# Earlier scale steps, sooner operands and one split in the first token-MLP of an interleaved GFNet and Mixer kernel

## The chip, the cores and the metric

The kernel runs on one core of a Trainium2 chip. The metric is the device time of one execution in microseconds (us). Three runs of the kernel before took 987.86, 980.19 and 978.45 us; their median is 980.19.

A core has five engines that run side by side, each through its own queue in order: TensorE (PE, matrix products, with PEld for loading its weights), VectorE (DVE), ScalarE (ACT), GpSimd (POOL) and SyncE (SP), which here only issues transfers. An engine waits for another through semaphores, and everything queued behind a waiting instruction waits too.

## The reference

Four layers with residuals follow each other on x of 2048 tokens by 640 channels: a spectral filter, a token-mixing MLP, and the same two again with the same weights.

```python
def _A_ref(x, w_r, w_i):
    B, S, D = x.shape
    X = rfft2(x, axes=(-2, -1))
    X = X * (w_r + 1j * w_i)
    return irfft2(X, s=(S, D), axes=(-2, -1))

def _B_ref(x, w1, b1, w2, b2):
    h = _layernorm(x, axis=-1)                  # (1, 2048, 640)
    u = jnp.einsum("bsd,sf->bdf", h, w1) + b1   # F = 1728
    u = _gelu(u)
    y = jnp.einsum("bdf,fs->bds", u, w2) + b2
    return y.transpose(0, 2, 1)

x = A_x
x = x + _A_ref(_layernorm(x, axis=-1), A_w_r, A_w_i)
x = x + _B_ref(_layernorm(x, axis=-1), B_w1, B_b1, B_w2, B_b2)
x = x + _A_ref(_layernorm(x, axis=-1), A_w_r, A_w_i)
x = x + _B_ref(_layernorm(x, axis=-1), B_w1, B_b1, B_w2, B_b2)
```

## The kernel before

The spectral filter is done as matrix products with tables (tM, tD, tS, tI). Products that need float32 are made from float16 parts: an operand is scaled by a power of two and split into a high half (written by ACT) and a low half, the rest (written by DVE as one scalar_tensor_tensor of source, scale and high half). One product is then three passes: high by high, high by low, low by high.

The change is all in `b1st`, the token-MLP of the first round. It has two parts. The first contracts the 2048 tokens with w1 into 1728 hidden rows, in 14 weight tiles of 128 rows (`NFT`; the last half-filled); the second contracts the hidden rows with w2 into 2048 tokens, in 16 tiles (`NJ`). Tiles are numbered through: 0 to 13 are w1, 14 to 29 are w2.

Tiles 0 to 3 of w1 are done plainly (`both`: 48 steps of two matmuls of 128x320, the three passes). The other ten are five pairs (4 and 5, 6 and 7, and so on), and each pair is done in the manner of Strassen: seven products of block sums in place of eight. The table `ops` lists 35 such products as (pair, name): first A11 and A12 of the first and second pair, then S1, S2, S4, S3, A22 of both, then all seven of the third, fourth and fifth pair. The weight operand of each comes from raw w1 blocks and their sums X (`ssum`), the activation operand from blocks and sums T1 to T4 of h (`tsum` forms them in place on DVE, `thi` writes the high half on ACT, `tlo` the low half on DVE). `product(n)` issues 24 matmuls. `work(n)` issues what stands around it: it evicts product n−1, splits the weight of product n+3 (`hi` on ACT, `lo` on DVE, with a store of the split weight on POOL's queue for the second round), forms the sum for product n+4, and then runs the closures listed in `todo[n]`. `work(-4)` to `work(-1)` run inside `both` of tile 3.

A weight scale is a power of two from the sum of squares. `wload(m)` loads a tile (two transfers of raw weights, by SP). `scan1(m)` is ACT's Square with a sum per partition (`junk<-raw`). `scale1(m)` is a generator with three steps, each taken by `step(m)`: first DVE adds the partial sums up into `sqb`; second PE multiplies `ones` with it, which puts the sum on all partitions; third five small DVE operations make the power of two (`s1p`, `c1p` for pairs, `st`, `ct` for tiles of w2). The second and third step of a pair stand at the table `mms` inside a product, those of the second pair in `both` at j == 32.

For w2, `wsplit(m)` writes `wh` on ACT and `wl` on DVE, in two halves of 896 columns. Tile 14 is split from `todo`, tile m+1 during product m. Each product of w2 is evicted as a row x (128 tokens by 640), whose layernorm for the next spectral layer follows: statistics on DVE, `r` and `nb` on POOL, `z` on ACT, folds on POOL and DVE (`eo`, `f`), a split (`fh`, `fl`) and a product with tM. Between the products stand the split of the next tile, scans and scale steps, and loads, at fixed places of the inner loop (`i`).

Order: each engine's instructions run in the order of its queue. From the start of `b1st` until after the last `ulo`, `self.pin` is true, and every instruction is kept in the order in which the code is written. After that, except in the last three rows, a scheduler sets the order of each engine from its estimates. All instructions go through the wrapper `Pin`, so the profile gives them one line, L83, and they are told apart by engine and tile.

Of the kernel before, what the change touches and what calls it, by code (L numbers as in the profile page):

```python
# [21 lines left out]
NJ, NG, NFT = 16, 16, 14  # L22
# [32 lines left out]
PAIR = 4  # L55
# [35 lines left out]
class Layers:  # L91
# [965 lines left out]
    def b1st(self, li):  # L1057
# [9 lines left out]
        prod, tsum, thi, tlo, hlow, hhigh, hlows = H.prod, H.tsum, H.thi, H.tlo, H.hlow, H.hhigh, H.hlows  # L1067
# [7 lines left out]
        def step(m):  # L1075
            if m in sc:
                next(sc[m])
# [11 lines left out]
        def ssum(d, a):  # L1089
            if a == "S1":  # L1090
                X[d] = self.t(self.pX, [128, 8, 128], F32, "X", 1)
            x, y, op = {"S1": ("A21", "A22", ADD), "S2": ("S1", "A11", SUB), "S3": ("A11", "A21", SUB), "S4": ("A12", "S2", SUB)}[a]
            V.tensor_tensor(src(d, a), src(d, x), src(d, y), op=op)

        begin, rest = ("A11", "A12"), ("S1", "S2", "S4", "S3", "A22")
        ops = [(d, a) for ds, q in (((0, 1), begin), ((0, 1), rest)) for d in ds for a in q]
# [7 lines left out]
        def hi(n):  # L1104
            if 0 <= n < len(ops):
                d, a = ops[n]
                q, tag = places(n)
                wo[n] = self.t(q, [128, NJ, 128], F16, tag, 1).rearrange("p (a b) c -> p a b c", a=2)
                T.activation(wo[n][:, 0], src(d, a), AF.Identity, scale=self.s1p[:, d:d + 1])

        def lo(n):
            if 0 <= n < len(ops):
                d, a = ops[n]
                V.scalar_tensor_tensor(wo[n][:, 1], src(d, a), self.s1p[:, d:d + 1], wo[n][:, 0], op0=MUL, op1=SUB)
                nc.gpsimd.dma_start(self.ws1[d][a], wo[n])
# [12 lines left out]
        def gelu(o, x=None, **q):  # L1128
            T.activation(o, o if x is None else x, AF.Gelu_apprx_tanh, **q)

        def evict(n):
            if not 0 <= n < len(ops):
                return
            (d, a), ps = ops[n], bank[n]
            c = self.c1p[:, d:d + 1]
            if a == "A11":
                f[d] = self.t(pf, [128, 4, 320], F32, "f", 4)
            to = f[d]
            if a in ("A11", "S1"):
                for i in (0, 2) if a == "A11" else (3,):  # L1140
                    T.activation(to[:, i], ps, AF.Identity, scale=c)
            else:
                i, k = {"S2": (2, 2), "S4": (1, 2), "S3": (2, 2), "A12": (0, 0), "A22": (2, 2)}[a]
                V.scalar_tensor_tensor(to[:, i], ps, c, to[:, k], op0=MUL, op1=ADD)
            if a in ("S4", "S3"):
                i, k = (1, 3) if a == "S4" else (3, 2)
                V.tensor_tensor(to[:, i], to[:, i], to[:, k], op=ADD)

        def evicted(n):
            if n > 0 and ops[n][1] in ("S4", "A22"):  # L1150
                d, k = ops[n][0], 2 * (ops[n][1] == "A22")
                gelu(f[d][:, k:k + 2], bias=self.b1[:, d + 7 * k // 2:d + 7 * k // 2 + 1])

        def work(n, more=()):

            evict(n - 1)
            hi(n + 3)
            d, a = ops[n + 4] if 0 <= n + 4 < len(ops) else (0, "A11")
            if a in ("S1", "S3", "S4"):
                ssum(d, a)  # L1160
            lo(n + 3)
            if a == "S2":
                ssum(d, a)
            evicted(n - 1)
            for e in more:
                e()
# [4 lines left out]
        def uhi(e, i=0, k=4):  # L1171
            T.activation(U[e][:, 0, i:i + k], fu(e)[:, i:i + k], AF.Identity, scale=self.su)

        def ulo(e, i=0, k=4, c=slice(0, 128)):
            h, l = (U[e][c, q, i:i + k] for q in range(2))
            V.scalar_tensor_tensor(l, fu(e)[c, i:i + k], self.su[c], h, op0=MUL, op1=SUB)
# [46 lines left out]
        def plain(m, o, x):  # L1223
            i = SEQ[m]
            gelu(o, x, scale=self.ct[0][:, i:i + 1], bias=self.b1[:, i:i + 1])
# [33 lines left out]
        def both(ps, w):  # L1259
            for k, (i, h) in enumerate(((0, hhigh), (0, hlows), (1, hhigh))):  # L1260
                for j in every:
                    yield k * NJ + j
                    prod(ps, w[i], h, [j], start=k == 0, stop=k == 2)

        for j in both(ps, w):
            pass
        plain(2, f[5][:, 0:2], flat(ps))
        ps, w = self.big(), self.w.pop(3)
        self.wstore(3, w)
# [2 lines left out]
        todo = collections.defaultdict(list)  # L1272
        lam = lambda g, *a, **k: lambda: g(*a, **k)
        for d in range(2, 5):
            a, b, n = 2 * d + PAIR, 2 * d + PAIR + 1, 7 * d
            for m, c, q, k in ((a, 0, "S3", 3), (a, 1, "S4", 2), (b, 0, "S3", 2), (b, 1, "A22", 2)):
                todo[at[d - 2, q] - k].append(lam(self.wload, m, (c,)))
            for k, m, c in ((9, a, 0), (8, a, 1), (8, b, 0), (7, b, 1)) if d == 2 else ((11, a, 0), (10, a, 1), (9, b, 0), (7, b, 1)):
                todo[n - k].append(lam(self.scan1, m, (c,)))
            for k in (6, 5) if d > 2 else (5, 4):  # L1280
                todo[n - k].append(lam(step, a))
        one = PAIR + 2
        for q in one, one + 1:
            self.wload(q)
        todo[-4] += [lam(self.scan1, one), lam(tlo, "T1"), lam(thi, "T3")]
        todo[-3] += [lam(self.scan1, one + 1), lam(tlo, "T2")]
        todo[-2] += [lam(step, one)]
        todo[0] += [lam(tlo, "T3")]
        todo[1] += [lam(tsum, "T4", 0), lam(tsum, "T4", 1), lam(thi, "T4")]
        todo[3] += [lam(tlo, "T4")]  # L1290
        a, b = NFT, NFT + 1
        for n, m, c in ((22, a, 0), (23, b, 0), (24, a, 1), (25, b, 1), (31, a + 2, 0), (31, a + 2, 1), (32, a + 3, 0), (32, a + 3, 1)):
            todo[n].append(lam(self.wload, m, (c,)))
# [5 lines left out]
        for k, e in enumerate((0, 6, 5, 1, 2, 3)):  # L1299
            todo[25 + k].append(lam(uhi, e))  # L1300
            todo[26 + k].append(ulast if e == 6 else lam(ulo, e))
        todo[32] += [lam(self.wopen, a), lam(self.wsplit, a, (0,))]
        todo[33] += [lam(self.wsplit, a, (1,))]
        todo[34] += [lam(uhi, 4, 0, 2), lam(ulo, 4, 0, 2)]
        mms = {7 * d - 4 - (d > 2): 2 * d + PAIR for d in range(2, 5)}
        mms.update({30: a, 34: b})

        for j in both(ps, w):
            if j % 12 == 0:
                work(j // 12 - 4, todo[j // 12 - 4])  # L1310
            if j == 32:
                step(one)
                step(one)
        plain(3, f[5][:, 2:4], flat(ps))
        for n in range(len(ops)):
            if n == 5:
# [4 lines left out]
            work(n, todo[n])  # L1321
        evict(len(ops) - 1)
        evicted(len(ops) - 1)
        uhi(4, 2, 2)
        ulo(4, 2, 2)
        step(NFT + 2)
        self.pin = False
        for a in ("f", "fr", "T", "h", "ha"):
            self.pop(a)
# [48 lines left out]
        for j in range(NJ):  # L1378
# [42 lines left out]
            def sum5(a):  # L1421
                x = X[5], px5[0]
                o, x, op = (X[5], x if a < "S3" else x[::-1], ADD if a == "S1" else SUB)
                with self.after(evicted5):
                    V.tensor_tensor(o, *x, op=op)
                nc.sync.dma_start(self.ws1[5][a], o)
# [10 lines left out]
            for i, (ft, a, k) in enumerate(order):  # L1437
                if i == 14 and w5[:1] > ("",):
                    sum5(w5[0])
                if i == 20:  # L1440
                    for q in w5[1:]:
                        load5(q)
                if tail and i == NFT:
                    half(0)
                if j == NJ - 2 and i in (4, 20):
                    flush(1)
                if j >= NJ - 2 and i in (6, 12, 17):
                    next(row)
                if tail and i == 2:
                    self.wopen(0)  # L1450
                    self.wsplit(0, lo=False)
                if i in (4, 8):
                    next(steps, None)
                if j == NJ - 3 and i == 9:
                    self.wload(0)
                if i in ((6, 7) if j else (18, 19)):
                    step(m + 2)
                if i in (15, 18):
                    self.scan1(m + 3, (i // 3 - 5,))
                if i == 26 and m + 3 < NFT + NJ:  # L1460
                    step(m + 3)
                o = pss[a][:, :320]
                if not j:
                    first(o, ft, a, k)
                elif ft < NFT - 1:
                    self.mm3(o, (wh[:, ft], wl[:, ft]), (upart(ft, a, 0), upart(ft, a, 1)), ft == SEQ[0], ft == SEQ[-1])
                else:
                    mm(o, wh[:, ft], upart(ft, a, 1), start=False, stop=False)
                    mm(o, wl[:, ft], upart(ft, a, 0), start=False, stop=False)
# [722 lines left out]
```

## Time and profile before

| what | value |
|---|---|
| median of three runs | 980.19 us (978.45 to 987.86) |
| the profiled execution, its time | 984.12 us |
| its span on the core | 982.3 us |
| mean granted TensorE clock | 0.979 |
| PE busy | 934.8 us, 95% |
| DVE busy | 754.8 us, 77% |
| ACT busy | 565.5 us, 58% |
| POOL busy | 293.3 us, 30% |
| DMA moved | 179.42 MB, 183 GB/s on average |

A timeline row gives start, duration, engine, operation, out<-in with shapes, how many, and in brackets how long the engine had been idle and what ended that. Rows that say "x16" are merged. "sqTrue" and "sqFalse" are sums of squares of a pair and of a single tile. In the first token-MLP the weights of the Strassen products are called `wo`, `wh` or `wl` by the place that holds them, so there `wh<-raw` on DVE is a low half too.

### The profile page before, as it was taken

To read this page: it belongs to the slowest core of one execution; us is meant where nothing else is said; L and a number is where in the kernel's file an instruction comes from. 1 tells how busy PE (TensorE), PEld (TensorE's weight loads), DVE (VectorE), ACT (ScalarE), POOL (GpSimd) and SP (SyncE) were. 2 spreads that over 40 slices of the span, in tenths; PEclk is the share of its full clock that TensorE was granted. 3 is DMA by queue.
4 is the path that set the end of the run, shared out by engine and by line. 5 is a ranking of instruction groups with operands and counts; after the bars stand their busy time and mean duration, and the time that the engine had idled before them with its cause. 6 is when DMAs were issued, how large, how long until landed. Compare 5 with 4: busy or idle time off the path is not lost.

```text
span 982.3 us, 22469 instructions
## 1 busy us (share of the span) xinstructions
PE 934.8 (95%) x9009; PEld 691.2 (70%) x9009; DVE 754.8 (77%) x1407; ACT 565.5 (58%) x869; POOL 293.3 (30%) x496
## 2 busy tenths in 40 slices
PE   3889899999999989999999898999999999999998
PEld 2768777666677767777777686776777777777776
DVE  7979989987988956666667897889735455988885
ACT  5847879884676674555544476684433344454431
POOL 6939867311111112122223495772000000000000
PEclk9599999998999999999999999999999999999999
DMA  7856377642887685664332663674555447655411
GB/s 259 284 153 173 107 238 237 220 171 88 297 306 243 230 314 190 214 201 130 111 93 81 173 194 123 206 242 158 165 163 160 143 132 274 219 192 176 146 48 52
DMA packets 68108, 179.42 MB, mean 183 GB/s; under 512 B 8010, under 2 KB 15332, under 8 KB 68004
## 3 DMA queue, kind: packets, MB, share of 16 engines
q1 hardware_dynamic: 60820, 151.63, 47.6%
q0 software_dynamic: 7184, 26.36, 7.3%
q8 instruction: 70, 1.15, 0.5%
q14 instruction: 34, 0.28, 0.1%
HBM read 130.39 MB, written 47.58 MB: 181 GB/s over the span
## 4 chain that ended last, share of the span: by engine, by line
PE 49%; DVE 24%; ACT 9%; POOL 7%; issue 6%; DMA 5%; SPq 1%; ACTq 0%; DVEq 0%; POOLq 0%
PE ps L83 49%; DVE f L83 4%; DVE wl L83 3%; DVE st L83 3%; POOL eo L83 3%; DMA raw<-w 2%; DVE s1l L83 2%; DMA xt<-x 2%; ACT wh L83 2%; ACT junk L83 2%; ACT z L83 1%; DVE xt L83 1%; DVE Yl L83 1%; POOL xt L83 1%; POOL xl L83 1%
## 5 line engine op out<-in xcount | busy, mean ns | idle before, releaser
L83 PEld LDWEIGHTS <-wh 128*128 128x128 f16 x2298 | 222.4, 98 | 89.3 <-issue 1.7
L83 PE MATMUL ps<-u,wh 128*128 128x320 f16 x1242 | 228.5, 299 | 0.7 <-ACT wh L83 0.7
L83 PEld LDWEIGHTS <-wl 128*128 128x128 f16 x1626 | 159.9, 99 | 69.6 <-issue 5.6
L83 PE MATMUL ps<-u,wl 128*128 128x320 f16 x826 | 182.1, 299 | 0.1
L83 PEld LDWEIGHTS <-wo 128*128 128x128 f16 x924 | 90.3, 98 | 35.9 <-issue 0.9
L83 POOL TENSOR_TENSOR r<-v,mh 128x1 f32<-128x1 f32 x64 | 39.3, 613 | 147.7 <-DVE nm L83 138.4
L83 PE MATMUL ps<-tDi,Yh 128*128 128x322 f16 x320 | 72.4, 304 | 1.5 <-ACT Yh L83 1.5
L83 ACT ACTIVATE junk<-raw 128x896 bf16<-128x896 f32 (+1 forms) x60 | 59.4, 991 | 13.1 <-DMA raw<-w 11.0
L83 DVE TENSOR_TENSOR f<-eo 128x256 f32<-128x256 f32 (+1 forms) x124 | 39.0, 367 | 36.2 <-POOL eo L83 35.6
L83 POOL TENSOR_TENSOR xt<-xt,ec 128x320 f32<-128x320 f32 x64 | 53.3, 853 | 31.8 <-DVE xt L83 31.7
L83 DVE BATCH_NORM_STATS2 st<-xt 128x6 f32<-128x320 f32 x126 | 55.2, 480 | 5.1 <-DMA xt<-x 4.5
L83 PE MATMUL ps<-u,wo 128*128 128x320 f16 x420 | 58.8, 299 | 0.0
L83 ACT ACTIVATE z<-xt,nb,r 128x640 f32<-128x640 f32 x31 | 28.5, 918 | 52.5 <-POOL z L83 43.2
L83 PE MATMUL ps<-tM,f 128*128 128x128 f32 x160 | 37.6, 402 | 21.5 <-DMA xt<-x 11.4
L83 PE MATMUL ps<-tDi,Yl 128*128 128x322 f16 x192 | 56.4, 302 | 1.4 <-DVE Yl L83 1.4
L83 DVE SCALAR_TENSOR_TENSOR wl<-raw,s,wh 128x896 f16<-128x896 f32 (+2 forms) x43 | 48.0, 1123 | 12.6 <-ACT wh L83 12.4
L83 POOL TENSOR_TENSOR eo<-z 128x320 f32<-128x320 f32 x60 | 52.2, 892 | 17.3 <-ACT z L83 15.3
L83 PEld LDWEIGHTS ps<-tM,f 128*128 128x128 f32 x160 | 31.5, 283 | 27.3 <-DVE f L83 26.8
L83 POOL TENSOR_TENSOR xl<-ta,xh 128x642 f16<-128x642 f32 (+2 forms) x34 | 45.5, 1347 | 4.6 <-ACT xh L83 4.5
L83 ACT ACTIVATE wh<-raw,s 128x896 f16<-128x896 f32 (+2 forms) x46 | 43.7, 987 | 2.6 <-DVE s L83 1.8
L83 POOL MEMSET wl<- 64x256 f16 x2 | 0.6, 306 | 146.7 <-DMA wl<-w2A 146.7
L83 PE MATMUL ps<-hhb,wh 128*128 128x320 f16 x256 | 43.5, 299 | 0.4 <-ACT hhb L83 0.4
(257 smaller groups left out, 2222.9 us busy)
## 6 DMA issues: line engine op xcount, KB each, us to landing
xt<-x SPq DMA_DIRECT2D x79, 320.0 KB
raw<-w SPq DMA_DIRECT2D x32, 512.0 KB
w<-w SPq DMA_DIRECT2D x48, 321.0 KB
x<-xt SPq DMA_DIRECT2D x47, 320.0 KB
raw<-w SPq DMA_DIRECT2D x32, 448.0 KB
raw<-w2z SPq DMA_DIRECT2D x32, 448.0 KB
out<-xt SPq DMA_DIRECT2D x15, 320.0 KB
w1S<-wl POOLq DMA_DIRECT2D x9, 512.0 KB, 5.8
```

The costliest lines, as they stand in the source:

```text
L83: i = f(*a, **k)
```

## The change

It has four parts, and adds or removes no instruction on any engine.

1. The second pair (tiles 6 and 7). Its loads are issued before `both` of tile 2 instead of after, and the scan of tile 6 stands ahead of the eviction of tile 2 on ACT. In `both` of tile 3 `work(-4)` to `work(-1)` stand at j = 0, 12, 32, 36 instead of 0, 12, 24, 36; the first scale step of the pair and the sum S1 of the first pair are issued with `work(-3)` instead of `work(-2)` and `work(0)`; the high half of T3 comes behind the scans of tile 7, and T3's low half and T4's sums come two places sooner, T4's low half one.
2. The first scale step of the third pair comes one product sooner.
3. Both halves of tile 14 are split in `todo[32]`, where the second was in `todo[33]`.
4. The first scale step of tile 16 stands ahead of the last `uhi` and `ulo`, and its second and third step stand at i = 44 and 45 of the first product of w2 instead of 18 and 19.

```diff
-            d, a = ops[n + 4] if 0 <= n + 4 < len(ops) else (0, "A11")
+            d, a = ops[n + 4] if 0 < n < len(ops) - 4 else (0, "A11")
...
+        one = PAIR + 2
+        for q in one, one + 1:
+            self.wload(q)
         for j in both(ps, w):
             pass
+        self.scan1(one)
         plain(2, f[5][:, 0:2], flat(ps))
...
-            for k in (6, 5) if d > 2 else (5, 4):
+            for k in (6, 5) if d > 2 else (6, 4):
                 todo[n - k].append(lam(step, a))
-        one = PAIR + 2
-        for q in one, one + 1:
-            self.wload(q)
-        todo[-4] += [lam(self.scan1, one), lam(tlo, "T1"), lam(thi, "T3")]
-        todo[-3] += [lam(self.scan1, one + 1), lam(tlo, "T2")]
-        todo[-2] += [lam(step, one)]
-        todo[0] += [lam(tlo, "T3")]
-        todo[1] += [lam(tsum, "T4", 0), lam(tsum, "T4", 1), lam(thi, "T4")]
-        todo[3] += [lam(tlo, "T4")]
+        todo[-4] += [lam(tlo, "T1")]
+        todo[-3] += [lam(self.scan1, one + 1), lam(tlo, "T2"), lam(thi, "T3"), lam(step, one), lam(ssum, 0, "S1")]
+        todo[-2] += [lam(tlo, "T3")]
+        todo[-1] += [lam(tsum, "T4", 0), lam(tsum, "T4", 1)]
+        todo[1] += [lam(thi, "T4")]
+        todo[2] += [lam(tlo, "T4")]
...
-        todo[32] += [lam(self.wopen, a), lam(self.wsplit, a, (0,))]
-        todo[33] += [lam(self.wsplit, a, (1,))]
+        todo[32] += [lam(self.wopen, a), lam(self.wsplit, a)]
...
         for j in both(ps, w):
-            if j % 12 == 0:
-                work(j // 12 - 4, todo[j // 12 - 4])
             if j == 32:
                 step(one)
                 step(one)
+            if j in (0, 12, 32, 36):
+                n = {0: -4, 12: -3, 32: -2, 36: -1}[j]
+                work(n, todo[n])
...
+        step(NFT + 2)
         uhi(4, 2, 2)
         ulo(4, 2, 2)
-        step(NFT + 2)
...
-                if i in ((6, 7) if j else (18, 19)):
+                if i in ((6, 7) if j else (44, 45)):
                     step(m + 2)
```

The first place is ACT while PE works on tiles 2 and 3 of w1. Before, from the second half of T2h on (`junk` are the scans of tiles 6 and 7, `wo` and `wh` weights of the first products, `fr` the eviction of tile 2):

```order
L83 ACTIVATE T2h_3698<-hf_326_2845 128x1280
L83 ACTIVATE fr_522_3909<-ps_3968,b1s,c_74 128x640
L83 ACTIVATE junk,sqTrue_4077<-raw_4069 128x1024
L83 ACTIVATE junk,sqTrue_4077<-raw_4071 128x1024
L83 ACTIVATE T3h_3700<-hf_326_2842 128x1280
L83 ACTIVATE T3h_3700<-hf_326_2843 128x1280
L83 ACTIVATE wo_4108<-raw_3712,sp_79 128x1024
L83 ACTIVATE junk,sqTrue_4077<-raw_4073 128x1024
L83 ACTIVATE junk,sqTrue_4077<-raw_4075 128x1024
L83 ACTIVATE wh_4140<-raw_3714,sp_79 128x1024
```

and now:

```order
L83 ACTIVATE T2h_3698<-hf_326_2845 128x1280
L83 ACTIVATE junk,sqTrue_4073<-raw_3969 128x1024
L83 ACTIVATE junk,sqTrue_4073<-raw_3971 128x1024
L83 ACTIVATE fr_522_3909<-ps_3968,b1s,c_74 128x640
L83 ACTIVATE wo_4106<-raw_3712,sp_79 128x1024
L83 ACTIVATE junk,sqTrue_4073<-raw_3973 128x1024
L83 ACTIVATE junk,sqTrue_4073<-raw_3975 128x1024
L83 ACTIVATE T3h_3700<-hf_326_2842 128x1280
L83 ACTIVATE T3h_3700<-hf_326_2843 128x1280
L83 ACTIVATE wh_4168<-raw_3714,sp_79 128x1024
```

Tile 6's scans moved ahead of the eviction, and T3h from between the two tiles' scans to behind them; `wo` stands ahead of tile 7's scans in place of T3h.

The same place on DVE, with - for before and + for now (`sqb` is the sum of the second pair, `X` the sum S1 of the first pair, `qt` the first of the scale's small operations, which reads PE's result):

```order
-L83 SCALAR_TENSOR_TENSOR wo_4108<-raw_3712,sp_79,wo_4108 128x1024
+L83 SCALAR_TENSOR_TENSOR wo_4106<-raw_3712,sp_79,wo_4106 128x1024
 L83 TENSOR_TENSOR T2l_3699<-hf_326_2844,T2h_3698 128x1280
 L83 TENSOR_TENSOR T2l_3699<-hf_326_2845,T2h_3698 128x1280
-L83 SCALAR_TENSOR_TENSOR wh_4140<-raw_3714,sp_79,wh_4140 128x1024
-L83 TENSOR_REDUCE sqb_536_4144<-sqTrue_4077 128x1
+L83 TENSOR_REDUCE sqb_535_4116<-sqTrue_4073 128x1
+L83 TENSOR_TENSOR X_4118<-raw_3716,raw_3718 128x1024
 L83 TENSOR_SCALAR qt<-ps_3739 128x1
```

`sqb` now follows T2l directly, the low half of `wh` stands behind the scale's operations, and X is formed in the time between.

The second place is DVE around the last products of w1 (`wl_5390` are the two low halves of tile 14, `sqb_655` the sum of tile 15, `f` evictions):

```order
 L83 SCALAR_TENSOR_TENSOR f_5271<-ps_5321,cp_80,f_5271 128x320
 L83 SCALAR_TENSOR_TENSOR wl_5390<-raw_5016,s_73,wh_5389 128x896
+L83 SCALAR_TENSOR_TENSOR wl_5390<-raw_5088,s_73,wh_5389 128x896
 L83 SCALAR_TENSOR_TENSOR f_5271<-ps_5358,cp_80,f_5271 128x320
 L83 TENSOR_TENSOR f_5271<-f_5271 128x320
-L83 TENSOR_REDUCE sqb_655_5424<-sqFalse_5355 128x1
-L83 SCALAR_TENSOR_TENSOR wl_5390<-raw_5088,s_73,wh_5389 128x896
-L83 SCALAR_TENSOR_TENSOR f_5271<-ps_5393,cp_80,f_5271 128x320
+L83 TENSOR_REDUCE sqb_655_5426<-sqFalse_5355 128x1
+L83 SCALAR_TENSOR_TENSOR f_5271<-ps_5395,cp_80,f_5271 128x320
```

Tile 14's second low half moved ahead of an eviction, its addition and tile 15's `sqb`.

The third place is DVE at the start of the w2 stage. First the sum of tile 16 (`sqb_659`) against the low halves of tile 15 (`wl_5509`) and the last hidden rows (`u`):

```order
+L83 TENSOR_REDUCE sqb_659_5469<-sqFalse_5423 128x1
 L83 SCALAR_TENSOR_TENSOR wl_5509<-raw_5056,s_73,wh_5508 128x896
 L83 SCALAR_TENSOR_TENSOR wl_5509<-raw_5132,s_73,wh_5508 128x896
 L83 SCALAR_TENSOR_TENSOR u_554_4385<-f_5271,su,u_554_4385 128x640
-L83 TENSOR_REDUCE sqb_659_5471<-sqFalse_5421 128x1
-L83 TENSOR_REDUCE sqb_674_5579<-sqFalse_5546 128x1
```

`sqb_659` moved from behind these to ahead of them. Then the first row (`xt_5500`) against the low halves of tile 16 (`wl_5652`), where the scheduler sets the order:

```order
 L83 SCALAR_TENSOR_TENSOR wl_5652<-raw_5351,s_73,wh_5651 128x896
+L83 SCALAR_TENSOR_TENSOR xt_5500<-ps_5513,c_75,xt_5500 128x640
+L83 TENSOR_SCALAR q_671_5569<-ps_5675 128x1
 L83 SCALAR_TENSOR_TENSOR wl_5652<-raw_5353,s_73,wh_5651 128x896
-L83 SCALAR_TENSOR_TENSOR xt_5500<-ps_5513,c_75,xt_5500 128x640
-L83 TENSOR_SCALAR q_673_5578<-ps_5675 128x1
 L83 BN_STATS st_5617<-xt_5500 128x6 x2
```

The second low half of tile 16 moved from ahead of the row's eviction to between the eviction and the row's statistics. On SP the second load of tile 18 now stands ahead of the loads of tD, tS and tI, where it stood behind them. On PE the only move is the product of `ones` for tile 16, 16 matmuls later.

## The prediction

> **What bounds the kernel now.** I read the page first: the span, the busy shares and the shares of the chain that ended last.
>
> ```profile
> span 982.3 us, 22469 instructions
> PE 934.8 (95%) x9009; PEld 691.2 (70%) x9009; DVE 754.8 (77%) x1407; ACT 565.5 (58%) x869; POOL 293.3 (30%) x496
> PE 49%; DVE 24%; ACT 9%; POOL 7%; issue 6%; DMA 5%; SPq 1%; ACTq 0%; DVEq 0%; POOLq 0%
> ```
>
> TensorE (PE) is busy 95% of the span, so a reordering can win only PE's idle time or matmuls that run at half clock; 982.3 − 934.8 = 47.5 us are idle in all. The change touches one token-MLP, the first, so next come PE's waits between 175 and 400 us (us in total, times, longest), and PE by stretches (length, busy us and count of PE, PEld, DVE, ACT, POOL, then the granted clock, DMA share, GB/s).
>
> ```profile
> PE ps L83 <- DVE sqb L83: 6.1, 4, 3.2
> PE ps L83 <- ACT wh L83: 0.7, 1, 0.7
> ```
>
> ```profile
> 220.00:224.00 4.00, 2.14 (x10) 1.22 (x10) 2.73 (x10) 1.15 (x1) 0.53 (x1) 0.58 0.32 133
> 224.00:228.00 4.00, 4.00 (x18) 2.36 (x17) 2.42 (x2) 0.00 (x0) 0.53 (x1) 0.56 0.43 175
> 228.00:264.00 36.00, 35.91 (x265) 25.73 (x263) 31.95 (x31) 22.09 (x28) 4.78 (x9) 1.00 0.52 185
> 400.00:450.00 50.00, 50.00 (x409) 36.95 (x408) 30.66 (x87) 25.51 (x39) 11.29 (x24) 1.00 0.60 191
> ```
>
> The stage holds 6.8 us of waits that have a name: four times PE waited for `sqb`, the reduced sum of squares that its small matmul with `ones` spreads over the partitions to set a weight scale, and once for the high half of a weight (`wh`). A second loss is in the clock column: around the longest wait the granted clock is 0.58 and 0.56. From 400 to 450 PE never waits. So the prize lies between 218 and 354 us, and what becomes of it is settled in the w2 stage after it.
>
> **The change part by part.** It adds and removes no arithmetic; every price is a wait removed, a wait added, or a position in a queue. *First part, the second pair (tiles 6 and 7).* The timeline of before around the longest wait:
>
> ```profile
> 205.41 2.34 PE L83 MATMUL ps<-hha,wl 128*128 128x320 f16 x16
> 209.75 2.34 PE L83 MATMUL ps<-hha,wh 128*128 128x320 f16 x16
> 209.96 0.88 ACT L83 ACTIVATE fr<-ps,b1s,c 128x640 f32<-128x640 f32 x1 [1.90 <-PE ps L83]
> 210.74 1.04 ACT L83 ACTIVATE junk<-raw 128x1024 bf16<-128x1024 f32 x1
> 211.91 1.06 ACT L83 ACTIVATE junk<-raw 128x1024 bf16<-128x1024 f32 x1
> 212.96 2.41 ACT L83 ACTIVATE T3h<-hf 128x1280 f16<-128x1280 f32 x2
> 215.28 1.13 ACT L83 ACTIVATE wo<-raw,sp 128x1024 f16<-128x1024 f32 x1
> 216.32 1.04 ACT L83 ACTIVATE junk<-raw 128x1024 bf16<-128x1024 f32 x1
> 217.49 1.06 ACT L83 ACTIVATE junk<-raw 128x1024 bf16<-128x1024 f32 x1
> 217.65 2.88 DVE L83 TENSOR_TENSOR T2l<-hf,T2h 128x1280 f16<-128x1280 f32 x2
> 220.46 1.27 DVE L83 SCALAR_TENSOR_TENSOR wh<-raw,sp,wh 128x1024 f16<-128x1024 f32 x1
> 221.65 0.15 DVE L83 TENSOR_REDUCE sqb<-sqTrue 128x1 bf16<-128x4 f32 x1
> 221.86 0.16 PE L83 MATMUL ps<-sqb,ones 128*128 128x1 bf16 x1 [3.25 <-DVE sqb L83]
> 221.88 4.43 PE L83 MATMUL ps<-hha,wl 128*128 128x320 f16 x16
> 228.97 1.25 PE L83 MATMUL ps<-hha,wo 128*128 128x320 f16 x8
> ```
>
> PE arrived at 221.86 − 3.25 = 218.61. The four scans (`junk`) were long done; `sqb` was late because it stood on DVE behind T2l and a weight's low half, which had waited for ACT's T3h and `wo`. Now T3h (2.41) stands behind the scans and `wo` on ACT, and on DVE `sqb` follows T2l. How far that brings it hangs on when tiles 6 and 7 land. The landings aren't listed, but this is the DMA traffic from 200 to 220 in half-microsecond slices:
>
> ```profile
> GB/s 0 0 0 0 0 0 139 188 254 279 336 352 369 401 410 401 320 123 188 156 213 262 180 295 311 336 393 262 123 33 0 0 0 0 0 0 0 0 319 393
> ```
>
> The dip to 123 at 208.5 parts tile 6's loads from tile 7's, and nothing moves from 215 to 219, so all of tile 7 has landed by about 215. Tile 6's second half landed between the dip and 211.91, when its scan began; I take the middle, 210.2. Forward on ACT: second scan with its read-out to 211.5, eviction 212.4, `wo` 213.5; on DVE its low half (1.27) to 214.8, T2l 217.7, `sqb` 217.8, some 0.8 us ahead of PE; tile 7's last scan ends near 216.4. Bounds: none of the wait stays; or, with tile 6 at 211.91, all that slides by 1.7 us and a stall of about 1.0 stays. I take all: −3.25. The clock: the 32 matmuls on the `wl` half took 209.75 − 205.41 = 4.34 us for tile 2 and 228.97 − 221.88 = 7.09 here, with nothing waited for in between: −2.75 if the idle time that caused it is gone. Together −6.00. The rule in the Trainium skill, page "TensorE: Matmul & The Clock Gate", section "Part 1: The HAM clock gate (the "warmup" mystery)", is that the gate halves the rate only after at least one idle window of about 3.4 us, in a window that runs free. By that an idle time of 3.25 us would cost no clock and this part be worth 3.25; the stretch with 0.58 right behind that wait disagrees, so the measured 2.75 is in the sum.
>
> *T3 and T4 sooner* cost nothing on PE if DVE keeps ahead. DVE is busy 31.95 of 36 us between 228 and 264, where the first pair's products of 24 matmuls run at 4.34 × 24/32 = 3.26 us each; with PE 6 us sooner, T3l, X and the T4 sums stand ahead of the low halves that PE wants third and fourth. In order: scale steps done at 220.1, `wh` low 221.4, T3l 224.3, `wl` low 225.6; PE wants that `wl` at 228.97 − 6.0 + 2 × 3.26 = 229.5. Cover 3.9 us; if it went, the price would be what DVE is late.
>
> *Second part, one operation earlier for the third pair.*
>
> ```profile
> 263.22 1.27 DVE L83 SCALAR_TENSOR_TENSOR wl<-raw,sp,wl 128x1024 f16<-128x1024 f32 x1
> 264.42 0.15 DVE L83 TENSOR_REDUCE sqb<-sqTrue 128x1 bf16<-128x4 f32 x1
> 264.62 0.16 PE L83 MATMUL ps<-sqb,ones 128*128 128x1 bf16 x1 [0.71 <-DVE sqb L83]
> ```
>
> `sqb` stood behind a low half of 1.27; moved ahead of it and of an eviction it saves more than the wait: −0.71, all of it.
>
> *Third and fourth part, into the w2 stage.*
>
> ```profile
> 342.76 0.15 DVE L83 TENSOR_REDUCE sqb<-sqFalse 128x1 bf16<-128x2 f32 x1
> 343.10 0.17 PE L83 MATMUL ps<-sqb,ones 128*128 128x1 bf16 x1
> 345.62 5.88 PE L83 MATMUL ps<-u,wh 128*128 128x320 f16 x42 [0.70 <-ACT wh L83]
> 351.89 1.15 DVE L83 SCALAR_TENSOR_TENSOR wl<-raw,s,wh 128x896 f16<-128x896 f32 x1 [0.55 <-ACT wh L83]
> 353.76 0.21 DVE L83 TENSOR_REDUCE sqb<-sqFalse 128x1 bf16<-128x2 f32 x2
> 353.96 0.16 PE L83 MATMUL ps<-sqb,ones 128*128 128x1 bf16 x1 [1.92 <-DVE sqb L83]
> ```
>
> Splitting both halves of tile 14 in one step puts the second `wh` ahead of a gelu and two scans: the wait of 0.70 goes. It also puts the second low half (1.15) ahead of tile 15's `sqb`, which was ready at 342.91 for a matmul at 343.10, 0.19 in hand: a new wait of 1.15 − 0.19 = +0.96 (bounds 0, if DVE has gained time by then, and 1.15). Tile 16's `sqb` now stands ahead of both low halves of tile 15 (351.89 is the second) and the last `u`, and its matmul 16 matmuls later: it is ready two low halves (2.3) sooner and wanted 16 matmuls (2.2) later, 4.5 us against a wait of 1.92: −1.92, with 2.6 in hand. On SP the second load of tile 18 now stands ahead of the tables (tD, tS, tI, tM) and of x's first rows; it needs the buffer that tile 14's second low half frees, which ends sooner than before: 0, at worst that half's 1.15, with row 0 behind it. Sum on PE: −3.25 − 2.75 − 0.71 − 0.70 + 0.96 − 1.92 = **−8.4**.
>
> *What reaches the end.* Behind it sixteen products share a stage with a chain of normalisation and split through DVE, POOL and ACT.
>
> ```profile
> 360.99 0.83 ACT L83 ACTIVATE xt<-xt,b2s 128x640 f32<-128x640 f32 x1 [1.03 <-DMA xt<-x]
> 361.85 0.88 DVE L83 SCALAR_TENSOR_TENSOR xt<-ps,c,xt 128x640 f32<-128x640 f32 x1 [0.57 <-ACT xt L83]
> 362.77 0.89 DVE L83 BATCH_NORM_STATS2 st<-xt 128x6 f32<-128x320 f32 x2
> 430.68 0.92 ACT L83 ACTIVATE z<-xt,nb,r 128x640 f32<-128x640 f32 x1 [3.38 <-POOL z L83]
> 491.87 0.92 ACT L83 ACTIVATE z<-xt,nb,r 128x640 f32<-128x640 f32 x1 [3.38 <-POOL z L83]
> PEld L83 <- DVE wl L83: 0.6, 2, 0.4
> ```
>
> Five rows apart, `z` comes every (491.87 − 430.68)/5 = 12.24 us. PE is never idle from 400 to 450, and in the waits from 400 to 500 it begins to wait for `wl`: by the stage's end the chain, not PE alone, gives the pace, so the end moves with the chain's start. That is row 0's eviction and statistics. They move with PE and the loads that follow it, but in the new order the second low half of tile 16 stands between the eviction and the statistics (1.15, less what little waited there): +1.1. So −8.4 + 1.1 = **−7.3** reaches the end. The layers behind it are not reordered.
>
> **The rivals.** *PE alone decides* (chance 0.20): the chain has slack left, the +1.1 is hidden. For: PE 100% busy until 450. Against: it waits for `wl` afterwards. Then −8.4, with the new wait also gone −9.3: 970.9 to 971.8 for the median of 980.19.
>
> *The load is late* (0.08): tile 6 lands at the far bound, 1.0 us of the wait stays: −6.3, 973.9; with the half clock too, −3.5, 976.7. Against: no traffic after 215.
>
> *The clock loss isn't the wait's* (0.10): by the skill's rule 3.25 us idle is too little; the half-clock window then falls on some other moment. Worked from the rows: −7.3 + 2.75 = −4.6, 975.6. For: a wait of 1.92 at 354 is followed by no such stretch. Against: the drop sits directly behind the longest wait of the stage.
>
> *The gain is hidden* (0.08): a later stage waits on something that hasn't moved (a load, a store), 978 to 981. For: DMA is 5% of the chain. Against: everything issued behind this stage waits for its outputs or buffers.
>
> *DVE takes the wait's place, the slower side* (0.07): with T3l, X and T4's sums (2.88 + 1.22 + 2.88) ahead of low halves, DVE can't serve PE's earlier start. It decides from the point where the second `wl` low half ends later than the third product begins, i.e. over 3.9 us later than worked above. If DVE then gives back the whole 3.25 and PE idles long enough there for a second half-clock stretch: −0.71 − 0.70 − 1.92 from the other waits, −2.75 + 2 × 2.75 on the clock, +0.96 +1.1: the sum is +1.5, 981.7; over 1% slower would take a further 0.8 us on each of the first ten products.
>
> **How the numbers follow.** The profiled execution took 984.12 (span 982.3 and 1.8 around it); the runs are 987.86, 980.19 and 978.45, so it lies 0.4% above the median. 984.12 − 7.3 = 976.8; the same difference from the median gives 980.19 − 7.3 = **972.9**. The main case has 0.47: its own range, with the new wait 0 to 1.15, row 0's cost 1.1 to 1.25 and 0.15% (1.5) for the runs, is 970.4 to 974.7. The range over cases, 968 to 978.5, takes in PE alone below, the clock and late-load cases above, and leaves out the upper half of "hidden", DVE, and runs as far apart as those of before (1%). About 1% is what a measurement of this kernel can tell from no change: 9.8 us, or below 970.4. The main case is 0.7%; only PE alone with the new wait gone and a kind median gets there: faster 0.17. Slower, above 990, needs the DVE case at its worst: 0.05. Same: 0.78.
>
> **What would show it.** Right: no `sqb` in PE's waits between 200 and 355 but one of 0.8 to 1.1 for tile 15 near 336; the granted clock 1.00 from 205 to 260; the `wl` half that took 7.09 takes 4.3; the first product on `wo` begins at about 223 and not 228.97; in the w2 stage `z` still every 12.2, starting about 7 us sooner. Wrong: a clock of 0.6 again anywhere before 355 (the clock rival); waits for `wl` or `wh` between 225 and 260 (DVE); `z` rows 8 or more sooner (PE alone, or row 0's cost is hidden); a span shorter by under 4 us with all waits gone (hidden).

## The result, and the profile after

The changed kernel takes 976.33 us (median of 20 runs, 973.87 to 980.21); the kernel before, 20 runs beside it, 982.58 (977.68 to 987.86). The ratio is 0.9934, 95% interval 0.992 to 0.9948: 6.5 us less (5.1 to 7.9), inside the 1% that the prediction called the same. Forecast were 7.3 us less. The profiled execution took 974.83, with a span of 973.1 and a mean clock of 1.0. The page of the changed kernel, and PE's waits between 175 and 400 us:

```profile
span 973.1 us, 22470 instructions
PE 932.0 (96%) x9009; PEld 691.0 (71%) x9009; DVE 754.3 (78%) x1407; ACT 564.6 (58%) x869; POOL 293.4 (30%) x496
PE 55%; DVE 21%; ACT 8%; POOL 7%; issue 5%; DMA 3%; SPq 0%; ACTq 0%; DVEq 0%; POOLq 0%
```

```profile
PE ps L83 <- DVE sqb L83: 1.6, 2, 0.8
```

The two spans differ by 9.2 us, more than the kernels do. 1.9 of it lies ahead of the change: tile 2's pass on `wl` begins at 205.41 in the profile before and at 203.50 here. The first profile ran from 22.7 to 50 us at a clock of 0.50 and this one at 1.00, but that doesn't explain it: of the twelve profiles of this document, those with about 0.50 there begin the pass between 203.27 and 205.41, those with 1.00 between 203.28 and 209.47. Another 1.0 lies behind the last w2 product, where the twelve take 443.5 to 447.0 us. Both are scatter that the change doesn't touch; why the starts differ stays open. Places are therefore counted from the start of that pass. The timeline of the changed kernel, around the longest wait of before:

```profile
203.50 2.34 PE L83 MATMUL ps<-hha,wl 128*128 128x320 f16 x16
208.91 1.06 ACT L83 ACTIVATE junk<-raw 128x1024 bf16<-128x1024 f32 x1 [1.71 <-DMA raw<-w]
209.96 0.87 ACT L83 ACTIVATE fr<-ps,b1s,c 128x640 f32<-128x640 f32 x1
210.73 1.14 ACT L83 ACTIVATE wo<-raw,sp 128x1024 f16<-128x1024 f32 x1
213.10 2.88 DVE L83 TENSOR_TENSOR T2l<-hf,T2h 128x1280 f16<-128x1280 f32 x2
215.91 0.15 DVE L83 TENSOR_REDUCE sqb<-sqTrue 128x1 bf16<-128x4 f32 x1
216.54 0.17 PE L83 MATMUL ps<-sqb,ones 128*128 128x1 bf16 x1
220.91 1.25 PE L83 MATMUL ps<-hha,wo 128*128 128x320 f16 x8
```

`sqb` ends at 216.06, 0.48 us ahead of PE, which no longer waits. The second scan of tile 6 does wait for its load, as the prediction's bound feared, but the load lands early enough. The next rows are the third and the fourth pair's product of `ones`, tile 15's, and then row 0 of the w2 stage:

```profile
255.69 0.17 PE L83 MATMUL ps<-sqb,ones 128*128 128x1 bf16 x1
276.26 0.16 PE L83 MATMUL ps<-sqb,ones 128*128 128x1 bf16 x1 [0.83 <-DVE sqb L83]
335.93 0.16 PE L83 MATMUL ps<-sqb,ones 128*128 128x1 bf16 x1 [0.75 <-DVE sqb L83]
...
344.58 1.75 SPq L333 DMA_DIRECT2D tM<-tM  x4
346.38 1.38 SPq L1358 DMA_DIRECT2D xt<-x  x3
351.88 0.83 ACT L83 ACTIVATE xt<-xt,b2s 128x640 f32<-128x640 f32 x1 [2.98 <-DMA xt<-x]
352.74 0.88 DVE L83 SCALAR_TENSOR_TENSOR xt<-ps,c,xt 128x640 f32<-128x640 f32 x1 [2.65 <-ACT xt L83]
353.67 1.15 DVE L83 SCALAR_TENSOR_TENSOR wl<-raw,s,wh 128x896 f16<-128x896 f32 x1
354.74 0.88 DVE L83 BATCH_NORM_STATS2 st<-xt 128x6 f32<-128x320 f32 x2
357.00 0.92 ACT L83 ACTIVATE z<-xt,nb,r 128x640 f32<-128x640 f32 x1 [0.99 <-POOL z L83]
```

The third pair's wait is gone and the fourth pair has a new one of 0.83; tile 15 has the forecast one, 0.75; tile 16 has none. Row 0 now waits 2.98 for its x row where it waited 1.03, and the low half stands between eviction and statistics. And PE, which never idled between 400 and 450 before, does so now (length, then busy us of PE first; the last columns are clock, DMA share and GB/s). The two rows behind it are the waits:

```profile
400.00:415.00 15.00, 14.14 (x114) 10.00 (x112) 8.89 (x24) 8.41 (x13) 2.59 (x6) 1.00 0.71 240
408.32 0.31 PE L83 MATMUL ps<-u,wl 128*128 128x320 f16 x1 [0.51 <-DVE wl L83]
409.52 0.31 PE L83 MATMUL ps<-u,wl 128*128 128x320 f16 x1 [0.35 <-DVE v L83]
```

Both are products on the two low halves of a weight tile, which DVE writes from 407.12 and from 408.31, each in 1.14 us, behind the statistics of a row. This is how a late row reaches PE.

### The profile page after: what moved, and what is told of

Same layout as the page of the kernel before. It is cut to its first block, busy times and chain, and to the rows that moved or that the text cites. A ratio compares the mean times of both kernels' runs of the same rounds, so it can differ in the third digit from the quotient of the medians.

```text
span 973.1 us, 22470 instructions
## 1 busy us (share of the span) xinstructions
PE 932.0 (96%) x9009; PEld 691.0 (71%) x9009; DVE 754.3 (78%) x1407; ACT 564.6 (58%) x869; POOL 293.4 (30%) x496
## 4 chain that ended last, share of the span: by engine, by line
PE 55%; DVE 21%; ACT 8%; POOL 7%; issue 5%; DMA 3%; SPq 0%; ACTq 0%; DVEq 0%; POOLq 0%
PE ps L83 55%; DVE f L83 4%; DVE wl L83 3%; POOL eo L83 3%; DVE st L83 3%; DVE s1l L83 2%; ACT wh L83 2%; ACT z L83 1%; DMA xt<-x 1%; ACT junk L83 1%; DVE xt L83 1%; DVE Yl L83 1%; POOL xl L83 1%; POOL ta L83 1%; DVE tb L83 1%
## 5 line engine op out<-in xcount | busy, mean ns | idle before, releaser
L83 PEld LDWEIGHTS <-wl 128*128 128x128 f16 x1626 | 158.8, 98 | 66.0 <-DVE wl L83 3.0
L83 DVE SCALAR_TENSOR_TENSOR u<-f,su,u 128x1280 f16<-128x1280 f32 (+2 forms) x26 | 25.5, 996 | 25.4 <-ACT u L83 25.2
```

Of the source, the lines that this page charges most:

```text
L83: i = f(*a, **k)
```

## The experiments

All places in this table are microseconds after the start of tile 2's `wl` pass in that kernel's own profile: the first product on `wo`, the product of `ones` for tile 17 (PE's entry into the w2 stage), the start of row 0's statistics and of its `z`, and the end of the last w2 product. The kernel before, again, and T2 twice were executed once each and have no ratio.

| kernel | pass starts at | first `wo` | `ones` of 17 | statistics | `z` | last w2 product | ratio, 95% interval |
|---|---|---|---|---|---|---|---|
| before | 205.41 | 23.56 | 155.09 | 157.36 | 159.8 | 331.87 | |
| before, again | 204.40 | 22.43 | 153.89 | 156.27 | 158.8 | 330.94 | |
| changed | 203.50 | 17.41 | 146.88 | 151.24 | 153.5 | 325.57 | 0.9934 (0.992 to 0.9948) |
| changed, again | 204.50 | 17.41 | 145.90 | 150.33 | 152.6 | 324.90 | 0.9956 (0.9939 to 0.9973) |
| first part alone | 204.41 | 17.41 | 148.41 | 150.86 | 153.1 | 325.01 | 0.9935 (0.9905 to 0.9965) |
| parts two to four | 203.37 | 20.82 | 150.19 | 154.85 | 157.1 | 329.45 | 1.0006 (0.9983 to 1.0029) |
| third part undone | 203.37 | 17.41 | 146.62 | 151.21 | 153.5 | 325.40 | 0.9935 (0.991 to 0.996) |
| statistics delayed | 204.81 | 17.42 | 146.62 | 155.45 | 157.7 | 330.36 | 0.9987 (0.9964 to 1.001) |
| T2 twice | 203.27 | 19.55 | 149.66 | 154.14 | 156.4 | 328.87 | |
| statistics first | 204.81 | 17.41 | 146.84 | 150.71 | 154.0 | 325.90 | 0.9907 (0.9875 to 0.9939) |
| x rows and statistics first | 209.47 | 17.41 | 146.60 | 148.19 | 151.6 | 323.44 | 0.9903 (0.9873 to 0.9933) |
| three orders altered | 203.28 | 17.41 | 146.30 | 146.12 | 151.2 | 323.30 | 0.9925 (0.9899 to 0.9952) |

**The first part alone.** The kernel before with the first part of the diff; against the changed kernel, the third and fourth part undone look like this (the second, and the place of tile 16's first step, likewise):

```diff
-        todo[32] += [lam(self.wopen, a), lam(self.wsplit, a)]
+        todo[32] += [lam(self.wopen, a), lam(self.wsplit, a, (0,))]
+        todo[33] += [lam(self.wsplit, a, (1,))]
...
-                if i in ((6, 7) if j else (44, 45)):
+                if i in ((6, 7) if j else (18, 19)):
```

> The first part of the change alone (second pair's loads, scans, sum and scale, T3, T4 and X), the other three parts as before. Theory of the prediction: the wait of 3.25 us and the half-clock stretch of 2.75 us go, so the first product on `wo` comes 6.0 us earlier against the start of the stage; the other three waits (0.71, 0.70, 1.92) are still there, row 0's statistics follow its eviction as before, and all of it reaches the end: 6.0 us, ratio 0.9939, hardly less than the whole change (0.9934). Rival, the clock loss isn't the wait's: 3.25 us, ratio 0.9967. Rival, part of the 6.0 is given back at later waits that grow: sqb waits of the third pair or of tile 16 longer than 0.71 and 1.92, ratio 0.996 to 0.998.

Its ratio is 0.9935, as large a gain as the whole change's, with an interval of 3.4 to 9.3 us. The first product on `wo` comes at 17.41 as in the changed kernel, PE enters the w2 stage 6.7 us sooner than in the first profile, row 0's statistics begin 6.5 sooner, and the last product of w2 ends 6.9 sooner. The waits of tile 16 (1.9) and for `wh` (0.7) are still there; that of the third pair is not the expected 0.71 but 0.19. Against this kernel the changed one enters the w2 stage 1.5 us sooner and ends its last w2 product 0.6 us later: the other three parts won time on PE that didn't arrive.

**Parts two to four without the first.** The kernel before with the other three parts of the diff.

> Parts two, three and four without the first. Theory of the prediction as the profile after corrects it: on PE -0.71 -0.70 -1.92 and +0.75 for tile 15's new wait, the third pair's 0.71 given back as a wait of 0.8 at the fourth pair (+0.8), and +1.1 between row 0's eviction and its statistics: -0.7 us reaches the end, ratio 0.9993 (0.998 to 1.0005). Rival, PE alone decides: -1.8 to -2.6 us, ratio 0.9975 to 0.998. The wait of 3.2 for the second pair's sqb with a granted clock near 0.6 behind it is there as before.

The ratio is 1.0006; its interval begins at 0.9983, just above the rival's 0.9975 to 0.998. The surprise was in the profile. The same wait for `sqb` is there and no clock is lost behind it:

```profile
219.82 0.16 PE L83 MATMUL ps<-sqb,ones 128*128 128x1 bf16 x1 [3.25 <-DVE sqb L83]
219.84 2.33 PE L83 MATMUL ps<-hha,wl 128*128 128x320 f16 x16
222.01 2.34 PE L83 MATMUL ps<-hhb,wl 128*128 128x320 f16 x16
```

Without the clock loss of the first profile (2.74), before would stand at 157.36 − 2.74 = 154.62 for row 0's statistics; here they stand at 154.85. On PE parts two to four bring 155.09 − 2.74 − 150.19 = 2.2 us; on row 0's chain (eviction, statistics, `z`, folds and split of the row) they bring nothing, it is 0.2 later.

**Row 0's statistics delayed.**

```diff
+            if not j:
+                for _ in range(8):
+                    V.tensor_scalar(xt, xt, 1.0, None, op0=ALU.mult)
```

> The changed kernel with eight DVE multiplications of row 0 by one, in place, between its eviction and its statistics (same values); nothing of PE's work waits for them but the next steps of the row. They should take 0.35 us each, 2.8 in all. Theory, the chain of normalisation and split sets the pace by the end of the w2 stage: z of row 0 starts 2.8 us later, the rows behind it stay 2 to 3 us later, PE waits for wl from then on and the end moves by 2 to 3 us against the changed kernel: ratio to the kernel before 0.9934 + 0.0025 = 0.996. Rival, PE alone decides: the delay is taken up within a few rows and the ratio stays 0.9934.

Each multiplication took 0.49 us, not 0.35, so the statistics came 4.2 us later. The last product of w2 came 4.8 later and the ratio rose by 0.0053, about 5.2 us. PE idles in the middle of the stage, 30 us and more behind the row (it was busy for 15.00 and 14.14 of these stretches in the changed kernel):

```profile
385.00:400.00 15.00, 12.97 (x102) 9.02 (x102) 9.89 (x28) 6.69 (x10) 3.80 (x7) 1.00 0.65 218
400.00:415.00 15.00, 12.78 (x102) 8.90 (x100) 8.91 (x22) 6.80 (x10) 3.30 (x6) 1.00 0.58 206
```

That is 2.03 + 2.22 us idle. PE's waits in this stage (345 to 530 us) add up to 4.6:

```profile
PE ps L83 <- DVE v L83: 1.8, 3, 0.7
PE ps L83 <- DVE wl L83: 1.4, 1, 1.4
PE ps L83 <- DVE qi L83: 0.8, 2, 0.4
PE ps L83 <- DVE s1l L83: 0.6, 2, 0.4
```

A few DVE operations on one row cost their full length: in the changed kernel PE waits for what DVE does for the rows and between them. That PE alone decides is refuted for it. The multiplications hold up the row and the low halves behind it on DVE alike, so this run doesn't part the two; the kernel with x's rows first, below, brings the row forward without any DVE work less, and PE's idle time goes.

**The third part undone.**

```diff
-        todo[32] += [lam(self.wopen, a), lam(self.wsplit, a)]
+        todo[32] += [lam(self.wopen, a), lam(self.wsplit, a, (0,))]
+        todo[33] += [lam(self.wsplit, a, (1,))]
```

> The changed kernel with the third part undone: tile 14's second half is split one product later again. Theory: tile 15's new wait (0.75) goes, the wait for wh (0.70) comes back, and row 0's statistics follow its eviction directly again, which the third part had undone (0.0 against 1.1 us of the second low half of tile 16): z starts 1.1 us earlier than in the changed kernel, and the time is 1.1 us shorter, ratio to the kernel before 0.9923. Rival, PE alone decides: no difference to the changed kernel, 0.9934.

A miss: no difference, neither in the ratio nor in `z` (153.5 in both). Two rows say why:

```profile
353.66 0.89 DVE L83 SCALAR_TENSOR_TENSOR xt<-ps,c,xt 128x640 f32<-128x640 f32 x1 [2.90 <-ACT xt L83]
354.58 0.89 DVE L83 BATCH_NORM_STATS2 st<-xt 128x6 f32<-128x320 f32 x2
```

The low half is out of the way, and the eviction begins 150.29 us after the pass instead of 149.24, because its x row is issued 1.0 us later and lands later; the statistics stand where they stood, 151.21 and 151.24.

**The kernel before again, and T2's low half formed twice.** The second kernel is the changed one with one edit:

```diff
-        ... lam(tlo, "T2"), lam(thi, "T3"), lam(step, one), ...
+        ... lam(tlo, "T2"), lam(tlo, "T2"), lam(thi, "T3"), lam(step, one), ...
```

> The kernel before once more, for its clock. In the first profile the 3.25 us wait for the second pair's sqb was followed by a half-clock stretch, in the profile of parts two to four without the first the same wait was not: the first product on wo came 23.56 and 20.82 us after tile 2's wl pass. Theory, the stretch depends on where the clock's own windows of 3.4 us stand against the wait: one of these two values again, nothing between, and the granted clock near 0.55 only with 23.5. Rival, the stretch belongs to the kernel before: 23.5 again.

> The changed kernel with T2's low half formed twice on DVE (same values), which puts the second pair's sqb 2.9 us later: 12.4 + 2.9 against PE's arrival at 13.0, so a wait of about 2.3 us. Theory, the wait costs its own length and now and then a half-clock stretch more: first product on wo 17.4 + 2.4 = 19.8 us after tile 2's wl pass (22.5 with the stretch), granted clock 1.00. Rival, DVE's cover of 3.9 us for the low halves of the first products is gone as well: further waits for wl, wh or T3 between there and the first pair's last product.

Of the kernel before, the second profile (PE's rows, then two stretches of the windows):

```profile
220.85 0.16 PE L83 MATMUL ps<-sqb,ones 128*128 128x1 bf16 x1 [3.25 <-DVE sqb L83]
220.88 3.94 PE L83 MATMUL ps<-hha,wl 128*128 128x320 f16 x16
226.83 1.25 PE L83 MATMUL ps<-hha,wo 128*128 128x320 f16 x8
```

```profile
217.00:220.00 3.00, 0.60 (x5) 0.29 (x3) 3.00 (x3) 1.67 (x3) 0.54 (x1) 1.00 0.42 175
221.00:224.00 3.00, 3.00 (x13) 1.66 (x11) 1.94 (x7) 1.15 (x1) 0.53 (x1) 0.50 0.45 180
224.00:228.00 4.00, 4.00 (x30) 2.87 (x29) 1.41 (x2) 0.97 (x2) 0.53 (x1) 0.98 0.31 131
```

Neither of the two values that were expected: 22.43, a clock of 0.50 for some 3 us after the wait and 22.43 − 20.82 = 1.61 us lost. One wait of 3.25 us, three profiles, three prices on top: 2.74, 1.61 and none. The traces say more. Within a profile the changes of the granted clock lie whole multiples of 3.413 us apart (in the first one from 22.70 to 50.01 is 8 of them, from there to 220.68 is 50). Cut along that raster, the stretches around the wait are, two each for the first profile, the second one, and parts two to four (PE's busy time comes second, the clock third from the end):

```profile
217.26:220.68 3.42, 1.35 (x10) 0.85 (x9) 3.42 (x4) 2.38 (x5) 0.54 (x1) 1.00 0.37 153
220.68:224.09 3.41, 2.23 (x10) 1.31 (x10) 2.14 (x9) 1.15 (x1) 0.53 (x1) 0.50 0.28 117
217.36:220.78 3.42, 0.24 (x2) 0.04 (x1) 3.42 (x4) 1.31 (x3) 0.20 (x1) 1.00 0.37 153
220.78:224.19 3.41, 3.34 (x14) 1.95 (x14) 2.14 (x8) 1.15 (x1) 0.53 (x1) 0.50 0.40 159
214.79:218.21 3.42, 1.78 (x14) 1.16 (x12) 3.42 (x3) 2.81 (x5) 0.54 (x1) 1.00 0.32 133
218.21:221.62 3.41, 1.80 (x15) 1.30 (x15) 2.48 (x9) 0.85 (x1) 0.53 (x1) 1.00 0.21 87
```

Where the wait fell mostly into one stretch, leaving PE 1.35 or 0.24 us of work in it, half clock followed; where it was split over two, with 1.78 and 1.80, none did. In the first profile half clock lasted two stretches (PE busy for 2.23 and 3.41), in the second one (3.34). Half of that work is 2.8 and 1.7 us, near the prices measured, 2.74 and 1.61. So the price hangs on where the wait falls on the raster. That is read from the traces and was not tried by shifting the wait, and it gives no sharp line: elsewhere 1.49 of 3.41 (first part alone, from 343.02) was not followed by half clock and 2.03 (before, from 53.42) was.

With T2l twice the wait was 1.97 us, the clock stayed at 1.00, and the first product on `wo` came at 19.55, the 2.1 us later that the wait and its product cost. None of the first pair's products waited. The delay passed on in full, and grew: PE entered the w2 stage 2.8 us later, the fourth pair's wait being 1.47 instead of 0.83, and the last product of w2 came 3.3 us later.

**Statistics first.** One instruction was to move behind the statistics:

```diff
+                if (m, c) == (NFT + 1, 1):
+                    self.wsplit(m + 1, (c,), lo=False)
+                    with self.after(self.lastst):
+                        self.wsplit(m + 1, (c,), hi=False)
...
```

> The changed kernel with one instruction moved: the second low half of tile 16 stands behind row 0's statistics and no longer between its eviction and them. Theory: the statistics begin 1.1 us sooner (150.1 against 151.2 us after tile 2's wl pass), all z as much, PE's idle 0.9 us between 400 and 415 goes, and the z of the fifteenth row comes 0.6 to 1.0 us sooner (320.2 to 320.6 against 321.2): 0.1% at the end, ratio 0.9925 to 0.993, too little to be told from 0.9934 by the time. Rival, PE alone: z of the last rows and PE unchanged.

A miss in the other direction. The statistics came 0.5 us sooner and `z` 0.5 later:

```profile
355.52 0.89 DVE L83 BATCH_NORM_STATS2 st<-xt 128x6 f32<-128x320 f32 x2
356.38 1.14 DVE L83 SCALAR_TENSOR_TENSOR wl<-raw,s,wh 128x896 f16<-128x896 f32 x1
357.44 0.20 DVE L83 BATCH_NORM_AGGREGATE mv<-st 128x2 f32<-128x12 f32 x1
```

The low half now stands ahead of the aggregation, which the row needs just as much. The ratio (0.9907) has an interval that holds the changed kernel's 0.9934; the last product of w2 came 0.3 later, as `z` would have it.

**x's rows ahead of tM.** The loads of the first two rows are written ahead of the four tM loads; the rest as in the last kernel.

```diff
         self.a0_open()
+        p = self.pT
...
+        xts = [load(0), load(1)]
         for q in range(4):
             self.a0_load_m(q)
```

> As the kernel with the statistics first, and the loads of x's first two rows are issued on SP ahead of the four tM loads. Theory: row 0's eviction waits for its x row, which lands 5.5 us after its issue because 2 MB of tM are ahead of it; ahead of them it lands some 3 us sooner, the statistics begin 3 to 4 us sooner (147 to 148 us), the chain has slack again and PE sets the pace: no idle of PE between 358 and 505, fifteenth z at 320.2 or sooner, 1.0 us better than the changed kernel and no more, since PE is the next bound: ratio 0.992 to 0.993. Rival, the load isn't what row 0 waits for: no change against the kernel with the statistics first.

The eviction begins at 145.47 instead of 149.24, the statistics at 148.19 (3.1 us sooner; the first low half of tile 16 stands between the two here), `z` 1.9 sooner, and the last product of w2 2.1 sooner; between 385 and 415 PE is busy throughout:

```profile
385.00:400.00 15.00, 15.00 (x122) 11.04 (x121) 9.82 (x29) 6.69 (x10) 4.63 (x9) 1.00 0.56 187
400.00:415.00 15.00, 15.00 (x131) 11.27 (x130) 8.95 (x25) 7.52 (x11) 2.68 (x8) 1.00 0.63 226
```

The x row was what row 0 waited for. (The four tM loads are 256 KB each by the page, 1 MB and not 2.) The ratio can't be told from the changed kernel's.

**Three orders altered, beside the changed kernel.** To the last kernel, with both low halves of tile 16 held back until after the row's `nm`, comes:

```diff
-        todo[32] += [lam(self.wopen, a), lam(self.wsplit, a)]
+        todo[32] += [lam(self.wopen, a), lam(self.wsplit, a, (0,)), lam(self.wsplit, a, (1,), lo=False)]
+        todo[33] += [lam(self.wsplit, a, (1,), hi=False)]
...
```

> The changed kernel with three orders altered: x's first rows loaded ahead of tM, both low halves of tile 16 behind row 0's statistics, and tile 14's second low half behind tile 15's sqb (its high half stays early). Theory: statistics of row 0 at about 146.4 us after tile 2's wl pass, tile 15's wait of 0.75 gone, PE not idle in the w2 stage, and the last product of w2 ends where PE alone puts it: 323.44 (x rows first) - 0.75 = 322.7, against 325.57 in the changed kernel, 2.9 us or 0.3% less: ratio 0.9905 where the changed kernel has 0.9934. Rival, PE already sets the pace with x rows first and the chain's further lead is worth nothing, and tile 15's wait comes back as another: 323.4.

> The changed kernel again, beside the last one on the same chip: last product of w2 at 325.6 us after tile 2's wl pass, row 0's z at 153.5, ratio 0.9934. Its distance to the other kernel of this call in the time tells whether 0.3% can be seen.

975.02 us against 977.60 of the changed kernel on the same chip: ratios 0.9925 and 0.9956, whose intervals overlap. Held against each other directly, six executions of 972.56 to 976.52 stand against eleven of 975.83 to 980.33. They hardly overlap, so that the version is probably better, by 0.3%. The last product of w2 ends at 323.30, and the rival named that number: tile 15's wait is gone, the fourth pair's was 1.17 in this profile, and `z` came hardly sooner than in the kernel before this one although the statistics did. It stood on ACT behind the bias of a later row, which waited for its load:

```profile
353.76 0.83 ACT L83 ACTIVATE xt<-xt,b2s 128x640 f32<-128x640 f32 x1 [1.56 <-DMA xt<-x]
354.50 0.91 ACT L83 ACTIVATE z<-xt,nb,r 128x640 f32<-128x640 f32 x1
```

## Why the prediction was right, and where its steps were off

**The first part, −6.00.** By place: 23.56 − 17.41 = 6.15, and the first part alone carries the whole result. But the sum was right with a term that isn't fixed. The wait of 3.25 is in every profile of a kernel without the first part; the 2.75 of the clock was the dearest of three prices, 2.74, 1.61 and 0. The gain of this part is thus 3.4 to 6.15 by the profile it is held against, and runs of before spread over 10 us, of the changed kernel over 6. That the sum held the dearest price and still came near the time is in part luck; how often each price falls due in the 20 runs isn't shown. The prediction took the row over the rule of the Trainium skill ("TensorE: Matmul & The Clock Gate", "Part 1: The HAM clock gate (the "warmup" mystery)"): no loss without a whole idle window of some 3.4 us. The measurements decide against it as it was used, since 3.25 us of idle time was followed by half clock in two of three profiles, and in the first one the clock fell at 220.68, 2.1 us after PE's last product had ended at 218.61, at the end of a stretch with 1.35 us of work. That the window runs free, which the same section states, agrees with the raster on which the three prices fall.

**Second part, −0.71.** The wait is gone (52.19 against 59.21 for that product, 0.87 more than the first `wo` had gained), but the step "−0.71, all of it" failed: 20 us later the fourth pair's `sqb` made PE wait 0.83. It wasn't a loss in every profile: in the changed kernel again it is below what the waits list, with the third part undone 0.62, with three orders altered 1.17. Between the two stand two scans that waited 2.5 us for loads in the changed kernel; in the changed kernel again such a scan waited 0.26 and no wait was listed, with the third part undone 1.7 us of waiting went with 0.62. Whether the loads set it wasn't tried. With the first part alone the third pair's wait was 0.19, so that little of the 0.71 was left to win.

**Third and fourth part.** The wait for `wh` and that of tile 16 went, and tile 15's new wait was 0.75 for a forecast 0.96. PE entered the w2 stage 155.09 − 146.88 = 8.2 us sooner; forecast were 8.4.

**What reaches the end, −7.3.** Measured at row 0's statistics −6.1, at its `z` −6.3, at the last product of w2 −6.3. Two things are in that step. The low half between eviction and statistics cost 354.74 − 353.67 = 1.07, as forecast. But the row didn't "move with PE": its eviction moved by 156.44 − 149.24 = 7.2 and not by 8.2, since its x row is loaded behind tM, whose loads were issued at 344.58, as the low half of the last `u` ended on DVE; that is the mis-sized term, 1.0 us. With the third part undone the low half's 1.07 was there again as a later landing, so that the two aren't to be added: parts two to four were worth 2.2 us on PE and nothing on the chain, and nothing in the time (1.0006).

**The rivals.** PE alone decides: refuted for the changed kernel by the delayed statistics. But the step behind the prediction's choice was drawn too sharply for the kernel before: from PE's entry (`ones` of tile 17) to the last product it takes 176.8 us there, 177.0 again, 176.6 with the first part alone, 176.8 and 177.0 in the two kernels with x's rows first, none of which let PE idle by more than 0.1 us in the stage. In the changed kernel it takes 178.7. Before, both were about level; the first part moved both; the others moved only PE and made the chain the slower one by 1.9 us. The late load stayed within its bound, 0.48 us in hand instead of 0.8. DVE never took the wait's place: no wait of PE for a low half is listed in the first pair's products. Nothing shows as hidden further on: the last w2 product came 6.3 us sooner, and the time is 6.5 less.

**The number.** 976.33 lies 3.4 above the forecast and within its range. 2.4 of that is the kernel before, whose median is 982.58 over 20 runs and was 980.19 over three; the rest is as much as the 1.0 of row 0, though the interval of the time (5.1 to 7.9) would hold 7.3 as well.

## What to carry to other kernels

Where a stage is carried by two paths that are about level, a cut is worth what it moves on the later one: here 2.2 us of PE's waits taken away just ahead of such a stage showed nothing in the time, 4 us of DVE operations behind the first row's eviction cost their full length, and the loads of two rows issued sooner brought the stage's end forward by 2.5 us (325.90 to 323.44). Follow a gain to the first thing that gates the next stage, and look at what that queues behind. Count places from a mark just ahead of the change when two profiles are compared: these differ by up to 6 us before the changed code begins. And do not take the clock price of a wait from one profile: here the same wait cost three prices.

## What the runs showed of the hardware

The same idle time of PE, 3.25 us, cost 2.74, 1.61 and 0 us of clock in three profiles; 1.97 us cost none in one. The granted clock changed on a raster of 3.413 us, and the price was half of PE's work in the stretches at half clock (5.64 and 3.34 us of it). A row of 320 KB landed 351.88 − 346.38 = 5.5 us after its issue behind four loads of tM; issued ahead of them, its eviction came 3.8 us sooner. An in-place multiplication of 128x640 float32 on DVE took 0.49 us.
